# Squared ReLU with the square and the copy both on ScalarE, and the second product's halves stored apart and added at the end

## The chip, the cores and the metric

One core of a Trainium2 chip runs the whole kernel. The metric is the device time of one execution in microseconds (us). The time before is the median of three runs, 927.74 us. One further execution was profiled; all durations, waits and idle times below come from it.

## What is computed

The input x has 2048 rows of 640 numbers. Each row is normalised (layer norm without weights) to xn. Two branches read xn:

```
qkv = xn @ wqkv                        # 640 x 1920; 32 heads of 20
s   = softmax(mask(q k^T / sqrt(20))) v @ wo     # causal, window of 256
r   = relu(xn @ w1 + b1)               # 640 x 1536
y   = (r * r) @ w2 + b2                # 1536 x 640
out = x + s * silu(y)
```

All of it is in 32-bit floating point. The kernel keeps that precision with matrix products of rounded operands: an operand is split into a high part (its value rounded to the matrix engine's 32-bit format) and a low part (the rest), and a product is taken as high x high, high x low and low x high.

## The kernel before

**Stages.** A first stage normalises x, transposes it into `xT`, and computes v and the first q and k columns. Then a loop of 268 steps (`for s in range(steps)`) runs the attention, 16 head pairs by 16 row tiles, one tile a step. TensorE has time left in each step, and a generator `filler()` fills it with other products, one piece at a time: first the remaining q and k columns (`qkps`), then the MLP, at last the output product with wo (`out_filler`, tile `wops`), most of which runs after the attention has ended.

**One attention step** issues, for the head pair: scores (`sps`, TensorE) whose row maxima VectorE takes (`junk`, `mt`, L505); transposed scores (`stps`, TensorE, L540), which ScalarE exponentiates (`p`, L546) and GpSimd masks (`p`, L547 and L549); a step later ScalarE copies the result to 16 bits (`ph`, L554); a step after that VectorE computes what the copy lost (`pl`, L560); then TensorE multiplies both with v (`ops`). Every fourth step ScalarE also handles the row maxima (`mrow`, L518 and L519) and evacuates `ops` (`osb`, L596). The scores live in two single-bank tiles, the transposed scores in one tile of two banks with no second copy: the next `stps` waits until the `p` before it has been read out.

**The MLP** runs in eight blocks, `blocks`: the hidden columns are taken in two halves `hf` (0, then 1), and for each half the rows in four blocks `b` of 512. In a block there is first a stretch of six products into PSUM tiles `hps` (th x fp), each evacuated by `evac`: ScalarE takes the relu from PSUM (L971), ScalarE squares it into the high part `hh` (L972); the PSUM bank is then counted free. `later(1.2, rest)` puts off the rest: VectorE squares the relu in place (L976), GpSimd subtracts the high part to give the low part `hl` (L977). Then comes a stretch of eight products into tiles `yps` (four row tiles x two column halves), read from `hh` and `hl`. Their evacuation differs by half: for `hf` 0 ScalarE copies `yps` to `ysb` (L1011), and it is stored in DRAM as `y_d[0]`; for `hf` 1 VectorE adds to it the earlier half, read back into `yin` (L935, L1009), and the sum is stored as `y_d[1]`. The products `qkps`, `hps`, `yps` share three PSUM banks.

**The output stage** takes the rows in eight units of two row tiles. For a unit it loads the attention output `ob` and `y_d[1]` as `yb`; GpSimd adds the bias b2 (L1093), ScalarE takes silu (L1123); TensorE transposes `ob` and multiplies with wo in four groups `wops`; VectorE multiplies a group with `yb` (L1144) and GpSimd adds x, loaded as `xres` (L1145); the row tile is stored.

**What sets the order.** The order of instructions on each engine is fixed when the program is written: `clock` is the writer's own count of TensorE time, `later` and `soon` place deferred work by it, and each engine then runs its list strictly in that order. All transfers are issued by SyncE, also in one order; an issue that must wait holds up those behind it.

Of the kernel before, what the change touches and what calls it, by code (L numbers as in the profile page):

```python
# [9 lines left out]
F32 = mybir.dt.float32  # L10
# [3 lines left out]
AF = mybir.ActivationFunctionType  # L14
ALU = mybir.AluOpType

P = 128
S = 2048
D = 640
# [3 lines left out]
NT = S // P  # L23
KC = D // P
NP = H // 2
NB = 4
# [32 lines left out]
def attn_mlp_kernel(ctx: ExitStack, tc, x, wqkv, wo, w1, b1, w2, b2, out):  # L59
    nc = tc.nc  # L60
# [24 lines left out]
    y_d = [dram.tile([P, NT, D], F32, name=f"y{i}") for i in range(2)]  # L85
# [31 lines left out]
    wgt = ctx.enter_context(tc.tile_pool(name="wgt", bufs=2))  # L117
# [19 lines left out]
    with tc.tile_pool(name="ph1v", bufs=2) as p1v, tc.tile_pool(name="ph1", bufs=2) as p1, tc.tile_pool(name="ph1x", bufs=4) as p1b, tc.tile_pool(name="ph1w", bufs=1) as p1w, tc.tile_pool(name="ph1t", bufs=2, space=PSUM) as p1t:  # L137
        xts = {}
# [136 lines left out]
        with tc.manual_schedule(engines={E_.PE, E_.Activation, E_.DVE, E_.Pool, E_.SP}):  # L275
# [90 lines left out]
            for w in "kq":  # L366
                ps = pat.tile([P, BT // 2], F32, tag="s", name="qkps")
# [263 lines left out]
    def later(wait, fn):  # L631
        tasks.append((clock[0] + wait, len(tasks), fn))
# [254 lines left out]
    def filler():  # L887
# [37 lines left out]
        ensure("10")  # L925
        blocks = [(0, (b + NB - 1) % NB) for b in range(NB)] + [(1, (b + NB - 2) % NB) for b in range(NB)]
        last = len(blocks) - 1
        order = [4 * b + tt for hf, b in blocks if hf for tt in range(4)]
        yins = {}

        def load_yin(i):
            if i < NT:
                t = order[i]
                yins[t] = wgt.tile([P, D], F32, tag="wgkh", name="yin")
                nc.sync.dma_start(yins[t], y_d[0][:, t, :])  # L935
        xb, its = [xT[p][NB - 1] for p in range(2)], []

        for n, (hf, b) in enumerate(blocks):
            if n % NB == 0:
                ensure(f"1{hf}")  # L940
            if n == NB - 1:
                w1t[1] = queue_w1(1)
                w2t[1] = queue_w2(1)
                shut.update(("11", "21"))
            if n == last:
                wo_part = queue_wo()
                shut.add("o")
            ensure_bulk(its)
            wt1 = w1t[hf]()
            hs, made, nxt = {}, set(), []  # L950

            def used(n=n, b=b, nxt=nxt):
                if n == NB - 1:
                    shut.discard("11")
                if n == last:
                    shut.discard("o")
                if n < last and blocks[n + 1][1] != b:
                    nxt.extend(load_xb(blocks[n + 1][1]))
            for th in range(2):
                for fp in range(NFH // 2):  # L960
                    yield from room()
                    ps = Acc(BT, "hps")

                    def evac(ps=ps, th=th, fp=fp, hs=hs, made=made):
                        hh = [stg.tile([P, BT], F32R, tag="stg", name="hh"),
                              stg.tile([P, BT], F32R, tag="stg", name="hl") if fp == 0 else wgt.tile([P, D], F32R, tag=f"wg{'kq'[fp % 2]}l", name="hl")[:, :BT]]
                        hs[th, fp] = hh

                        vload[0] += 0.5
                        r = at2.tile([P, BT], F32, tag="relu", name="relu")  # L970
                        nc.scalar.activation(r, ps.tile, AF.Relu)  # L971
                        nc.scalar.activation(hh[0], r, AF.Square)  # L972
                        ps.free(0.9)

                        def rest():
                            nc.vector.tensor_mul(r, r, r)  # L976
                            nc.gpsimd.tensor_sub(hh[1], r, f32(hh[0]))  # L977
                            made.add((th, fp))
                        later(1.2, rest)
                    fi = hf * NFH + 2 * fp  # L980
                    job = open_job(evac, *([used] if (th, fp) == (1, NFH // 2 - 1) else []))
                    mms = [(i, lin1(wt1, (wp * KC + c) * FHALF + (2 * fp + i) * P, P), xb[xp][:, c * BT + th * MT:c * BT + (th + 1) * MT]) for i in range(2) for c in range(KC) for wp, xp in ((0, 0), (0, 1), (1, 0))]
                    for m, (i, w_, x_) in enumerate(mms):
                        halves(job, ps, w_, x_, m == 0, m == len(mms) - 1, i * MT, MT)
                        if m in (0, 3 * KC):
                            one_half(job, ps, i, b1s, pick[:, fi + i:fi + i + 1].to_broadcast([P, MT]), i * MT, MT)
                        yield 0.1065
            if n % NB == 0:
                ensure(f"2{hf}")
            if n == NB:  # L990
                load_yin(0)
                load_yin(1)
            wt2 = w2t[hf]()
            for tt in range(4):
                t = b * 4 + tt
                place = [None]
                jobs = []

                def start(nh, hf=hf, t=t, place=place, idx=4 * (n - NB) + tt, end=n == NB - 1 and tt == 3, n=n, tt=tt):
                    sl = slice(nh * HALF, (nh + 1) * HALF)  # L1000
                    ps = Acc(HALF, "yps")

                    def evac():
                        vload[0] += 0.5
                        if not nh:
                            place[0] = wgt.tile([P, D], F32, tag="wgqh", name="ysb")
                        ysb = place[0]
                        if hf:
                            nc.vector.tensor_add(ysb[:, sl], ps.tile, yins[t][:, sl])  # L1009
                        else:  # L1010
                            nc.scalar.activation(ysb[:, sl], ps.tile, AF.Copy)  # L1011
                        ps.free(1.2)
                        if nh:
                            post(y_d[hf][:, t, :], ysb)
                            if hf:
                                del yins[t]
                                load_yin(idx + 2)
                            if end:
                                shut.discard("21")
                    return [ps, open_job(evac), 0]  # L1020

                def product(jb, nh, fc):
                    ps, job, _ = jb
                    while (tt // 2, fc // 2) not in made:
                        if state[2] < 10 ** 6:
                            yield None
                        elif tasks:
                            finish()
                        else:
                            drain(backlog, 1)  # L1030
                    for hp, wp in ((0, 0), (0, 1), (1, 0)):
                        jb[2] += 1
                        halves(job, ps, hs[tt // 2, fc // 2][hp][:, fc % 2 * MT + tt % 2 * P:fc % 2 * MT + (tt % 2 + 1) * P], lin1(wt2, (wp * NFH + fc) * D + nh * HALF, HALF), jb[2] == 1, jb[2] == 3 * NFH)
                        yield 0.133
                for nh in range(2):
                    yield from room()
                    job = start(nh)
                    for fc in range(NFH):
                        yield from product(job, nh, fc)
                if n == last and tt % 2:  # L1040
                    load(0)
                    load(1)
            if n < last and nxt:
                xb, its = nxt
            else:
                its = []
# [33 lines left out]
        return wo_part  # L1080

    def out_filler(wo_part):
        oT, xts = {}, {}
        b2t = wgt.tile([P, D], F32, tag="wgkl", name="b2t")
        nc.sync.dma_start(b2t, b2.partition_broadcast(P))

        def load_res(t):
            xts[t] = wgt.tile([P, D], F32, tag="wgkh", name="xres")
            nc.sync.dma_start(xts[t], x[t * P:(t + 1) * P, :])

        def transposes(u):
            ob, yb = ld[u]
            nc.gpsimd.tensor_add(yb, yb, b2t.unsqueeze(1).to_broadcast([P, 2, D]))  # L1093
            big = bigp.tile([P, KC * BT], F32R, tag="big", name=f"oT_{u}")
            oT[u] = big.rearrange("p (s c n) -> p s c n", s=2, c=KC)
# [14 lines left out]
                pending.append(evac)  # L1110

        load_res(0)
        for u in range(2 * NB):
            while u not in ld:
                load(u)
# [8 lines left out]
            for t2 in range(2):  # L1124
# [3 lines left out]
                for nh in range(2):  # L1128
# [8 lines left out]
                    yield from mm_group(ps, mms, 0.133)  # L1137
                    if nh == 0 and t + 1 < NT:
                        load_res(t + 1)
                    load(u + 1)  # L1140
                    load(u + 2)

                    def evac(ps=ps, sl=sl, t2=t2, nh=nh, res=res, xt=xt, t=t, yb=yb):
                        nc.vector.tensor_mul(res[:, sl], ps, yb[:, t2, sl])  # L1144
                        nc.gpsimd.tensor_add(res[:, sl], res[:, sl], xt[:, sl])  # L1145
                        if t == NT - 1:
                            post(out[t * P:(t + 1) * P, sl], res[:, sl])
                        elif nh:
                            post(out[t * P:(t + 1) * P, :], res)
# [115 lines left out]
```

## Time and profile before

| | |
|---|---|
| median of the runs (lowest to highest) | 927.74 us (927.52 to 932.7) |
| the profiled execution | 931.02 us, of which 929.3 us is the span from its first to its last instruction |
| busy: TensorE products / weight loads | 895.5 us / 857.7 us |
| busy: VectorE / ScalarE / GpSimd | 723.1 / 625.7 / 592.5 us |
| the MLP | from 275 us (first `hps`) to 832 us (last `ysb`) |
| the output stage | from 832 us to the end |

In the rows of the profile, PE is TensorE's products and PEld its weight loads, DVE is VectorE, ACT ScalarE, POOL GpSimd, SP SyncE; a name with q is an engine's own queue. `out<-in` names the tiles written and read. Behind `|` stand busy us and the mean ns of one instruction, then the time for which the engine sat idle just before them and what ended it. A busy share is a mean over stages with different limits, and a wait is put down to the instruction that came last.

### The profile page before, as it was taken

The page shows a single profiled execution, that of the slowest core. Times are in us where ns is not written, and L with a number is a line of the kernel's source. Part 1 is how long each engine was busy: PE and PEld are TensorE (multiplying, and loading weights), DVE is VectorE, ACT ScalarE, POOL GpSimd, SP SyncE. Part 2 cuts the span into 40 slices and gives each one's busy share as a digit, 9 for nine tenths or more (in the row PEclk, how much of TensorE's full clock was granted, in tenths as well). Part 3 has the DMA queues.
Part 4 walks back from the last instruction along what each step waited for, and adds up shares of the span by engine and source line. Part 5 has one row for each costly group of instructions (what it writes and reads, how often), then busy time and mean ns, then how long its engine had stood idle before and what let it go on. Part 6 is the DMA issues. An engine that isn't in the chain of part 4 may idle for free.

```text
span 929.3 us, 35638 instructions
## 1 busy us (share of the span) xinstructions
PE 895.5 (96%) x14464; PEld 857.7 (92%) x14464; DVE 723.1 (78%) x1717; ACT 625.7 (67%) x1048; POOL 592.5 (64%) x863
## 2 busy tenths in 40 slices
PE   8999999999999999999999999999999999889998
PEld 8999999999888999899999898899999899889998
DVE  6874368999899978968978989989988988762332
ACT  4443338787888877877878787868777768762221
POOL 6010005676647877958968777968868868864654
PEclk9999999999999999999999999999999999997999
DMA  7897877679786263362454445374563471173773
GB/s 265 305 386 273 239 240 273 217 248 287 224 263 189 59 214 103 73 209 68 142 181 124 108 134 135 98 227 131 154 175 103 116 238 53 39 235 115 271 283 118
DMA packets 105419, 169.97 MB, mean 183 GB/s; under 512 B 41336, under 2 KB 58920, under 8 KB 102696
## 3 DMA queue, kind: packets, MB, share of 16 engines
q1 hardware_dynamic: 105256, 167.70, 57.3%
q8 instruction: 114, 1.87, 0.9%
q14 instruction: 49, 0.40, 0.1%
HBM read 96.17 MB, written 70.91 MB: 180 GB/s over the span
## 4 chain that ended last, share of the span: by engine, by line
PE 69%; DVE 10%; issue 8%; POOL 5%; ACT 5%; DMA 3%; DVEq 0%; POOLq 0%; ACTq 0%; SPq 0%
PE yps L487 12%; PE ops L487 10%; PE hps L487 10%; PE qkps L487 9%; PE wops L655 8%; PE vps L232 8%; PE sps L497 5%; DVE junk L505 4%; PE stps L540 4%; PE qkps L209 3%; DVE pl L560 2%; ACT p L546 2%; POOL p L549 1%; POOL p L547 1%; DMA qs<-mrow 1%
## 5 line engine op out<-in xcount | busy, mean ns | idle before, releaser
L505 DVE CUSTOM_DVE_ANT_0 junk<-sps,mask 128x384 bf16<-128x384 f32 (+2 forms) x512 | 270.8, 529 | 73.1 <-PE sps L497 30.2
L546 ACT ACTIVATE p<-stps,ebias 128x768 f32<-128x768 f32 (+2 forms) x256 | 219.0, 856 | 113.3 <-PE stps L540 76.2
L560 DVE TENSOR_TENSOR pl<-p,ph 128x768 f16<-128x768 f32 (+2 forms) x256 | 273.1, 1067 | 12.2 <-PE ops L487 8.1
L547 POOL TENSOR_SCALAR_AFFINE_SELECT p<-p 128x256 f32<-128x256 f32 x256 | 173.0, 676 | 155.7 <-ACT p L546 150.1
L487 PE MATMUL yps<-w,hh 64*128 64x320 f32 x1536 | 253.8, 316 | 10.6 <-DVE ysb L1009 6.4
L487 PE MATMUL hps<-xb,w 64*128 64x256 f32 x2520 | 238.9, 285 | 0.6 <-issue 0.5
L487 PEld LDWEIGHTS hps<-xb,w 64*128 64x128 f32 x2520 | 224.9, 187 | 1.2 <-issue 0.6
L554 ACT ACTIVATE ph<-p 128x768 f16<-128x768 f32 (+2 forms) x256 | 203.2, 794 | 26.1 <-POOL p L549 25.0
L487 PEld LDWEIGHTS yps<-w,hh 64*128 64x128 f32 x1536 | 194.3, 186 | 15.0 <-DVE ysb L1009 8.0
L487 PE MATMUL ops<-vp,ph 64*128 64x61 bf16 x2880 | 201.8, 189 | 0.1
L487 PE MATMUL ops<-vp,pl 64*128 64x61 bf16 x2880 | 199.9, 188 | 0.3 <-DVE pl L560 0.3
L487 PE MATMUL yps<-w,hl 64*128 64x320 f32 x768 | 187.7, 314 | 0.0
L487 PEld LDWEIGHTS <-ph 64*128 64x128 f16 x2880 | 174.4, 94 | 4.9 <-PE sps L497 1.1
L487 PEld LDWEIGHTS <-pl 64*128 64x128 f16 x2880 | 175.5, 94 | 0.6 <-DVE pl L560 0.5
L497 PE MATMUL sps<-ks,qs 60*128 60x384 f32 (+2 forms) x512 | 127.6, 360 | 9.1 <-DVE mt L505 8.3
L549 POOL TENSOR_SCALAR_AFFINE_SELECT p<-p 128x256 f32<-128x256 f32 x224 | 129.1, 576 | 0.0
L487 PEld LDWEIGHTS yps<-w,hl 64*128 64x128 f32 x768 | 120.5, 186 | 0.0
L540 PE MATMUL stps<-qs,ks 62*128 62x384 f32 (+2 forms) x512 | 112.8, 345 | 3.2 <-DMA qs<-mrow 1.6
L487 PE MATMUL qkps<-xT,wgkh 64*128 64x512 f32 x320 | 102.5, 398 | 0.0
L487 PE MATMUL qkps<-xT,wgqh 64*128 64x512 f32 x320 | 102.3, 397 | 0.0
L497 PEld LDWEIGHTS sps<-ks,qs 60*128 60x128 f32 x512 | 70.5, 185 | 22.3 <-DVE mt L505 20.6
L540 PEld LDWEIGHTS stps<-qs,ks 62*128 62x128 f32 x512 | 67.2, 187 | 6.9 <-issue 2.6
(120 smaller groups left out, 1721.1 us busy)
## 6 DMA issues: line engine op xcount, KB each, us to landing
ks<-k_d SPq DMA_DIRECT2D x64, 240.0 KB
qs<-q_d SPq DMA_DIRECT2D x64, 240.0 KB
xb<-xs SPq DMA_DIRECT2D x12, 1280.0 KB
xs<-xT SPq DMA_DIRECT2D x8, 1280.0 KB
y<-ysb SPq DMA_DIRECT2D x32, 320.0 KB
k_d<-shm SPq DMA_DIRECT2D x19, 512.0 KB
q_d<-shm SPq DMA_DIRECT2D x19, 512.0 KB
v_d<-vt SPq DMA_DIRECT2D x8, 976.0 KB
```

The lines of the kernel that those rows point to most:

```text
L209: nc.tensor.matmul(ps, wt[:, c, :], xT[part][b][:, c * BT + t0:c * BT + t0 + n], start=m == 1, stop=m == 3 * KC)
L232: nc.tensor.matmul(ps, xT[xp][b][:, c * BT + t * P: c * BT + (t + 1) * P], wv[wp][:, c, nh * HALF:(nh + 1) * HALF], start=first and m == 0 ...
L487: return nc.tensor.matmul(out, a[r], b_[r], skip_group_check=True, **kw)
L497: nc.tensor.matmul(ss[hh][:, :nk], qs[i][o, q * P:(q + 1) * P], ks[i][o, k0 * P:k0 * P + nk], start=True, stop=True)
L505: nc.vector.tensor_tensor_reduce(out=junk[:, :nk], in0=ss[hh][:, :nk], in1=mask[:, 3 * P - nk:], scale=1.0, scalar=-3.0e38, op0=ALU.add, o ...
L540: nc.tensor.matmul(tps[:, hh, :n], ks[i][o, kb * P:(kb + 1) * P], qs[i][o, kb * P:kb * P + n], start=True, stop=True)
L546: nc.scalar.activation(p32[:, :, :n], tps[:, :, :n], AF.Exp, scale=SCALE, bias=ebias)
L547: nc.gpsimd.affine_select(p32[:, :, 0:P], p32[:, :, 0:P], pattern=[[0, 2], [1, P]], compare_op=ALU.is_ge, fill=0.0, base=0, channel_multip ...
L549: nc.gpsimd.affine_select(p32[:, :, 2 * P:], p32[:, :, 2 * P:], pattern=[[0, 2], [-1, P]], compare_op=ALU.is_gt, fill=0.0, base=0, channel ...
L554: nc.scalar.activation(ph[:, :, :n], p32[:, :, :n], AF.Copy)
L560: nc.vector.tensor_sub(pl[:, :, :n], p32[:, :, :n], ph[:, :, :n])
L655: nc.tensor.matmul(ps, a, b_, start=j == 0, stop=j == n - 1)
```

## The change

ScalarE now takes three instructions at each of the 48 evacuations of `hps`: the relu, the square (in place, 32-bit) and a copy that rounds it to the high part. VectorE no longer squares. The deferred part comes 0.4 us instead of 1.2 us of the writer's clock after the relu and now holds the square and the copy. ScalarE evacuates both halves of the second product, so `y_d[1]` holds the second half alone. The first half is read back only in the output stage: two loads of 128 x 640 for each unit into new tiles `y0`, and two more additions on GpSimd ahead of the bias. There the addition of x moves from GpSimd to VectorE.

```diff
-        order = [4 * b + tt for hf, b in blocks if hf for tt in range(4)]
-        yins = {}
-        def load_yin(i):
-            ...
-                nc.sync.dma_start(yins[t], y_d[0][:, t, :])
...
                         r = at2.tile([P, BT], F32, tag="relu", name="relu")
                         nc.scalar.activation(r, ps.tile, AF.Relu)
-                        nc.scalar.activation(hh[0], r, AF.Square)
                         ps.free(0.9)

                         def rest():
-                            nc.vector.tensor_mul(r, r, r)
+                            nc.scalar.activation(r, r, AF.Square)
+                            nc.scalar.activation(hh[0], r, AF.Copy)
                             nc.gpsimd.tensor_sub(hh[1], r, f32(hh[0]))
                             made.add((th, fp))
-                        later(1.2, rest)
+                        later(0.4, rest)
...
                         ysb = place[0]
-                        if hf:
-                            nc.vector.tensor_add(ysb[:, sl], ps.tile, yins[t][:, sl])
-                        else:
-                            nc.scalar.activation(ysb[:, sl], ps.tile, AF.Copy)
+                        nc.scalar.activation(ysb[:, sl], ps.tile, AF.Copy)
                         ps.free(1.2)
                         if nh:
                             post(y_d[hf][:, t, :], ysb)
-                            if hf:
-                                del yins[t]
-                                load_yin(idx + 2)
...
+        def load_y0(u):
+            y0s[u] = [wgt.tile([P, D], F32, tag="wgql", name="y0") for _ in range(2)]
+            for t, y0 in enumerate(y0s[u]):
+                nc.sync.dma_start(y0, y_d[0][:, 2 * u + t, :])
...
         def transposes(u):
             ob, yb = ld[u]
+            for t, y0 in enumerate(y0s.pop(u)):
+                nc.gpsimd.tensor_add(yb[:, t], yb[:, t], y0)
             nc.gpsimd.tensor_add(yb, yb, b2t.unsqueeze(1).to_broadcast([P, 2, D]))
...
         load_res(0)
+        load_y0(0)
...
                     if nh == 0 and t + 1 < NT:
                         load_res(t + 1)
+                    if (t2, nh) == (0, 1) and u + 1 < 2 * NB:
+                        load_y0(u + 1)
...
                         nc.vector.tensor_mul(res[:, sl], ps, yb[:, t2, sl])
-                        nc.gpsimd.tensor_add(res[:, sl], res[:, sl], xt[:, sl])
+                        nc.vector.tensor_add(res[:, sl], res[:, sl], xt[:, sl])
```

TensorE's list has the same instructions in the same order in both programs. The other lists move. ScalarE, in the first stretch of block 4, between two exponentials (`p`) of which the first also has the row maxima and `osb` behind it; before:

```order
L546 ACTIVATE p_14185<-stps,ebias 128x768
L518 ACTIVATE mrow<-stps 8x128
L519 ACTIVATE mrow<-mrow 8x128
L971 ACTIVATE relu<-hps 128x512
L972 ACTIVATE hh<-relu 128x512
L596 ACTIVATE osb<-ops 128x488
L554 ACTIVATE ph<-p_14109 128x768
L546 ACTIVATE p_14277<-stps,ebias 128x768
```

and changed:

```order
L546 ACTIVATE p_14185<-stps,ebias 128x768
L518 ACTIVATE mrow<-stps 8x128
L519 ACTIVATE mrow<-mrow 8x128
L963 ACTIVATE relu<-hps 128x512
L967 ACTIVATE relu<-relu 128x512
L968 ACTIVATE hh<-relu 128x512
L596 ACTIVATE osb<-ops 128x488
L554 ACTIVATE ph<-p_14109 128x768
L546 ACTIVATE p_14273<-stps,ebias 128x768
```

One instruction of 128 x 512 more stands ahead of `osb`, `ph` and the next `p`. In the changed list 13 of the 48 evacuations have their square and copy between two `p` that also have `mrow` and `osb` between them.

VectorE, at the first evacuations of block 0 (`p`, `ph` and `pl` belong to the attention):

```order
 L505 ISA junk,mt_100<-sps,mask 128x384
 L505 ISA mt_100 128x1
-L976 TENSOR_TENSOR relu<-relu 128x512
 L560 TENSOR_TENSOR pl<-p_5461,ph 128x768
 L505 ISA junk,mt_100<-sps,mask 128x384
```

The square is gone from between a row maximum and the `pl` behind it; nothing takes its place.

SyncE, in the output stage, the issues of one unit; before:

```order
L1089 DMA xres<-in_A_x_dram 128x640
L1065 DMA ob_21391<-o_87 128x2x640
L1066 DMA yb_21392<-y_84 128x1280
L620 DMA out_dram<-res 128x640
```

and changed (`y_83` is the stored first half, `y_21397` and `y_21398` are the new tiles):

```order
L1077 DMA xres<-in_A_x_dram 128x640
L1048 DMA ob_21377<-o_87 128x2x640
L1049 DMA yb_21378<-y_84 128x1280
L1073 DMA y_21397<-y_83 128x640
L1073 DMA y_21398<-y_83 128x640
L620 DMA out_dram<-res 128x640
```

The two new loads are queued behind `ob` and `yb`, which are for the unit after the next, while they themselves are for the next one.

More of the change, by code (lines that the diff above doesn't have):

```diff
@@ L927, in filler @@
         last = len(blocks) - 1
-        order = [4 * b + tt for hf, b in blocks if hf for tt in range(4)]
-        yins = {}
-        def load_yin(i):
-            if i < NT:
-                t = order[i]
-                yins[t] = wgt.tile([P, D], F32, tag="wgkh", name="yin")
-                nc.sync.dma_start(yins[t], y_d[0][:, t, :])
         xb, its = [xT[p][NB - 1] for p in range(2)], []
@@ L997, in filler, with start @@
                 jobs = []
-                def start(nh, hf=hf, t=t, place=place, idx=4 * (n - NB) + tt, end=n == NB - 1 and tt == 3, n=n, tt=tt):
+                def start(nh, hf=hf, t=t, place=place, end=n == NB - 1 and tt == 3, n=n, tt=tt):
                     sl = slice(nh * HALF, (nh + 1) * HALF)
@@ L1082, in out_filler @@
     def out_filler(wo_part):
-        oT, xts = {}, {}
+        oT, xts, y0s = {}, {}, {}
         b2t = wgt.tile([P, D], F32, tag="wgkl", name="b2t")
         nc.sync.dma_start(b2t, b2.partition_broadcast(P))
+        def load_y0(u):
+            y0s[u] = [wgt.tile([P, D], F32, tag="wgql", name="y0") for _ in range(2)]
+            for t, y0 in enumerate(y0s[u]):
+                nc.sync.dma_start(y0, y_d[0][:, 2 * u + t, :])
         def load_res(t):
```

3 lines of the change are left out of this document (removed).

## The prediction

> **What bounds the kernel now.** I read the page's busy shares and its chain of work first, then what TensorE waits for in the MLP, then the busy time of each engine by stretch.
>
> ```profile
> span 929.3 us, 35638 instructions
> PE 895.5 (96%) x14464; PEld 857.7 (92%) x14464; DVE 723.1 (78%) x1717; ACT 625.7 (67%) x1048; POOL 592.5 (64%) x863
> PE 69%; DVE 10%; issue 8%; POOL 5%; ACT 5%; DMA 3%; DVEq 0%; POOLq 0%; ACTq 0%; SPq 0%
> ```
>
> TensorE is busy for 96% of the span and carries 69% of the chain. No instruction of TensorE is added, removed or moved by this change, so the time can only change through how long TensorE stands waiting. The waits of its weight loads from 275 to 833 us, the MLP (engine and line that waited, releaser: total us, times, longest):
>
> ```profile
> PEld sps L497 <- DVE mt L505: 15.8, 37, 1.2
> PEld yps L487 <- DVE ysb L1009: 8.0, 6, 3.9
> PEld yps L487 <- ACT ysb L1011: 4.1, 7, 1.0
> PEld yps L487 <- ACT relu L971: 2.6, 4, 1.5
> PEld stps L540 <- ACT mrow L518: 2.6, 5, 0.6
> PEld stps L540 <- ACT p L546: 1.2, 4, 0.5
> ```
>
> VectorE makes TensorE wait 15.8 + 8.0 = 23.8 us, ScalarE 4.1 + 2.6 + 2.6 + 1.2 = 10.5 us. So all that VectorE could give back is 2.6% of the span. Why VectorE is late, and whether ScalarE has room, is read from the first stretches of the eight blocks (here block 4 and the sum of all eight), then from the second stretches of the first and of the last four blocks:
>
> ```profile
> core 0: us, PE busy (x) PEld busy (x) DVE busy (x) ACT busy (x) POOL busy (x), PEclk, DMA share, GB/s
> 559.00:598.00 39.00, 36.43 (x710) 34.19 (x706) 36.42 (x76) 32.65 (x54) 31.76 (x44) 0.96 0.35 91
> sum 287.00, PE 278.02 PEld 266.76 DVE 260.57 ACT 238.94 POOL 244.04; mean PE 34.75 PEld 33.35 DVE 32.57 ACT 29.87 POOL 30.50
> ...
> sum 129.00, PE 124.31 PEld 119.91 DVE 104.87 ACT 100.41 POOL 91.36; mean PE 31.08 PEld 29.98 DVE 26.22 ACT 25.10 POOL 22.84
> ...
> sum 127.00, PE 119.93 PEld 116.09 DVE 103.49 ACT 83.84 POOL 89.28; mean PE 29.98 PEld 29.02 DVE 25.87 ACT 20.96 POOL 22.32
> ```
>
> In the first stretches VectorE is busy 260.57 of 287 us, 91%, ScalarE 83%, GpSimd 85%. That is where the change takes from VectorE and gives to ScalarE.
>
> **The change, part by part.** The prices, from the groups by line:
>
> ```profile
> L971 ACT ACTIVATE relu<-hps 128x512 f32<-128x512 f32 x48 | 27.9, 580 | 0.3 <-PE hps L487 0.3
> L972 ACT ACTIVATE hh<-relu 128x512 fp32r<-128x512 f32 x48 | 30.3, 632 | 1.5
> L976 DVE TENSOR_TENSOR relu<-relu 128x512 f32<-128x512 f32 x48 | 38.3, 799 | 4.0 <-ACT hh L972 3.6
> L1009 DVE TENSOR_TENSOR ysb<-yps,yin 128x320 f32<-128x320 f32 x32 | 15.4, 481 | 6.0 <-PE yps L487 3.1 <-DMA y<-ysb 2.8
> L1011 ACT ACTIVATE ysb<-yps 128x320 f32<-128x320 f32 x32 | 13.4, 420 | 0.0
> ```
>
> *VectorE loses the squares:* 48 x 0.799 = 38.3 us. In the first stretches its load falls from 260.57 to 222 us, 77%. The row maximum that TensorE waits for is queued behind less, but a `pl` still has to wait for ScalarE's `ph`, which will come later than now. Bounds: nothing back, or all of the 15.8 us. I take a little over half, **-9**: 14 points of load are taken away, but the later `ph` gives a part back.
>
> *VectorE loses the second half's evacuation:* 32 additions of 0.481 become 32 copies of 0.420 on ScalarE, which in those stretches goes from 83.84 to 97.3 of 127 us, 77%. That is what it carries in the first four blocks (100.41/129 = 78%), where the same copies cost 4.1 us of waiting against 8.0 us for the additions. Bounds: 0 to -8; **-4**.
>
> *ScalarE gains one instruction an evacuation.* The square stays; the copy is new. The nearest row is L972 with 632 ns, and as it must wait for the square I add 0.04 us: 48 x 0.67 = 32 us. In the first stretches that makes 238.94 + 32 = 271 of 287 us, 94%: ScalarE takes the place that VectorE has at 91%. Whether TensorE feels it depends on how late an exponential may be. The exponentials in the MLP, the transposed scores, and one step of ScalarE in block 4 in order of time:
>
> ```profile
> L546 ACT ACTIVATE p<-stps,ebias 128x768 f32<-128x768 f32 x204 | 174.2, 854 | 89.2 <-PE stps L540 60.5 <-PE stps L512 24.4 <-DVE pl L560 2.4
> L540 PE MATMUL stps<-qs,ks 62*128 62x384 f32 x448 | 101.1, 357 | 3.2 <-DMA qs<-mrow 1.6 <-ACT mrow L518 1.3 <-ACT p L546 0.2
> ...
> 589.84 0.90 ACT L546 ACTIVATE p<-stps,ebias 128x768 f32<-128x768 f32 x1 [0.39 <-PE stps L512]
> 590.64 0.25 ACT L518 ACTIVATE mrow<-stps 8x128 f32<-8x128 f32 x1
> 590.92 0.31 ACT L519 ACTIVATE mrow<-mrow 8x128 fp32r<-8x128 f32 x1
> 591.14 0.57 ACT L971 ACTIVATE relu<-hps 128x512 f32<-128x512 f32 x1
> 591.75 0.63 ACT L972 ACTIVATE hh<-relu 128x512 fp32r<-128x512 f32 x1
> 592.28 0.56 ACT L596 ACTIVATE osb<-ops 128x488 f32<-128x488 f32 x1
> 592.74 0.83 ACT L554 ACTIVATE ph<-p 128x768 f16<-128x768 f32 x1
> 593.47 0.89 ACT L546 ACTIVATE p<-stps,ebias 128x768 f32<-128x768 f32 x1
> ```
>
> 204 exponentials in 558 us make a step of 2.73 us. A step holds 0.36 us of `stps` and 0.90 us of `p`; as `stps` has one tile only, the rest, about 1.4 us, is how late `p` may be before TensorE stands. In the step shown `p` to `p` takes 593.47 - 589.84 = 3.63 us: already 0.9 us late. With the copy it is 4.30, 1.57 late: TensorE stands, and `ph` and `osb` behind the copy are late by 0.67 too. The changed order has 13 such steps. Priced in full they cost 13 x 0.67 = 8.7 us. The other 35 evacuations have no `mrow` and `osb`: 3.63 - 1.0 + 0.67 = 3.3 us from `p` to `p`, 0.6 late, mostly hidden; 0.12 us each, 4.2 us, for those that meet a queue already late. Together **+13**. Bounds: 0, if the 89.2 us for which ScalarE sat waiting ahead of `p` take it all, and +32, if none of it is hidden. A check by likeness: the waits of `stps` for ScalarE are 2.6 + 1.2 = 3.8 us now and would be 16.8 us with ScalarE at 94%; VectorE at 91% costs 15.8.
>
> The Trainium skill's page ScalarE: Activation LUTs, section Rules for kernel authors, speaks against this part: it sends multiplications to VectorE and budgets about 0.3 us and 0.83 ns an element for an ACTIVATE. As an estimate from that page an instruction of 512 would take 0.72 us, the 48 copies 35 us instead of 32; this case's trace has 0.632 us, and the sum would be 1 us higher by the page.
>
> *The relu queues behind another evacuation's copy, and the bank it frees is late:* the 2.6 us of waits for `relu` grow; 0 to +5, **+2**. GpSimd's `hl` keeps its length; it waits for ScalarE instead of VectorE.
>
> *The output stage.* GpSimd gives up 32 additions of 0.876 us and gets 16 of 128 x 640; VectorE gets 32. Rows: the additions, GpSimd's price for 128 x 640, and around one unit the last load's issue, silu and the multiplication that needs it; then the last addition, and the stage's load.
>
> ```profile
> L1145 POOL TENSOR_TENSOR res<-res,xres 128x320 f32<-128x320 f32 x32 | 27.8, 876 | 35.1 <-DVE res L1144 35.1
> L1093 POOL TENSOR_TENSOR yb<-yb,b2t 128x1280 f32<-128x1280 f32 x8 | 23.6, 2952 | 3.4 <-PE yps L487 3.4
> L188 POOL TENSOR_TENSOR wv<-wvr,wv 128x640 fp32r<-128x640 f32 x5 | 7.7, 1567 | 0.0
> 869.57 0.44 SPq L1066 DMA_DIRECT2D yb<-y  x1
> 862.86 1.29 ACT L1123 ACTIVATE yb<-yb 128x1280 f32<-128x1280 f32 x1
> 869.05 0.49 DVE L1144 TENSOR_TENSOR res<-wops,yb 128x320 f32<-128x320 f32 x1 [1.88 <-PE wops L655]
> 925.52 0.86 POOL L1145 TENSOR_TENSOR res<-res,xres 128x320 f32<-128x320 f32 x1 [1.26 <-DVE res L1144]
> 850.00:929.00 79.00, 74.66 (x558) 73.98 (x558) 25.85 (x52) 17.14 (x27) 44.86 (x40) 0.99 0.60 210
> ```
>
> The new loads go out behind the `yb` of 869.57, at 870. With 4 to 6 us for `ob`, `yb` and themselves at the 210 GB/s of the stage or a little above, two additions of 1.57, the bias 2.95 and silu 1.29, `yb` is ready at 881.4 to 883.4. The unit it is for starts its multiplications one unit of 9.9 us after 869.05, at 879. VectorE is 2 to 4 us late; three PSUM banks let TensorE run on for two groups of 2.2 us. So TensorE just does not stand, with nothing to spare: 0 to +5, I take **+1**. At the very end the addition on VectorE, about 0.48 us, replaces 0.86: **-0.4**.
>
> The sum: -9 - 4 + 13 + 2 + 1 - 0.4 = **+2.6 us**. The profiled execution, 931.0 us with its span of 929.3, would become 933.6; it lies 3.3 us over the median, so on the median the forecast is 927.7 + 2.6 = **930.3 us**.
>
> Beside the sum stands the clock, by stretch (it is the value after POOL's busy time):
>
> ```profile
> 572.40:575.80 3.40, 3.40 (x34) 3.40 (x33) 2.83 (x9) 2.24 (x5) 1.61 (x3) 0.50 1.03 251
> 835.20:848.90 13.70, 12.63 (x84) 11.76 (x85) 3.94 (x9) 3.30 (x6) 5.49 (x5) 0.50 0.37 126
> ```
>
> After stalls the granted clock was halved for 3.4 us, and for 13.7 us where the output stage begins. One such 3.4 us more or less is worth 1.7 us; I count none.
>
> **The rivals.** *ScalarE becomes the bound (slower).* In block 4's first stretch, where weights are split as well, ScalarE has 32.65 + 6 x 0.67 = 36.7 of 39 us. If a late `ph` also holds VectorE's `pl`, and with it the next row maximum, the relief of 9 us shrinks to 2 and the 13 become 20: -2 - 4 + 20 + 4 + 1 - 0.4 = +18.6, **946 us**. It decides once the exponentials are over 1.4 us late in every third step. For it: 94%, and one tile for `stps`. Against it: 89.2 us of idle time ahead of `p`.
>
> *VectorE's relief pays (faster).* ScalarE's idle time takes the copies but for 3 us, 14 of the 15.8 us come back and 6 of the 8: -14 - 6 + 3 + 1 - 0.4 = -16.4, **911 us**. For it: VectorE is the fullest engine now. Against it: the copies fall into the very stretches where ScalarE has 17% left. The Trainium skill's GPSIMD Engine Reference, section Specifications, speaks for it: GpSimd shares its memory interfaces with VectorE instructions that have two inputs there, and the squares are such. By that rule GpSimd's masks would shorten as well; no row here separates it.
>
> *The output stage waits for the stored halves (slower).* If the loads need 10 us, TensorE stands 3 us in each of the six later units, less the 1 counted: **947 us**.
>
> *The moved order does nothing:* if the waits merely change their names, **928 us**; this lies within my forecast's own range.
>
> **How the numbers follow.** Forecast (near balance, 919 to 937): 0.47. ScalarE the bound: 0.29. Output stage: 0.06. VectorE's relief: 0.18. A measurement of this kernel can tell about 1%, 9.3 us, from no change: faster than 918.5 has 0.18, slower than 937 has 0.35, between 0.47. The range goes from 912 to 948 and takes in the sums of both larger rivals but for the outer half of the faster one.
>
> **What would show it.** Right: `sps` waits for `mt` fall to about 7 us between 275 and 833; `stps` waits for `p` and `mrow` grow from 3.8 to over 12; VectorE at 75 to 80% and ScalarE over 92% in the first stretches; no waits of `wops` for `res` after 850. Wrong: if `stps` waits stay under 6 us, the copies were hidden and the time falls; if `sps` waits stay over 12, VectorE was late for another reason than its squares.

## The result: slower by 1.5%, a faster MLP and a slower output stage

| | median, us | ratio to before (95% interval) |
|---|---|---|
| before | 929.23 (4 runs, taken beside the change) | |
| changed | 943.62 (4 runs) | 1.0146 (1.0106 to 1.0185) |

The profiled execution of the changed kernel took 944.62 us with a span of 942.5; before, 931.02 and 929.3. One execution of the first experiment's kernel ran at a granted clock of 0.654 and took 1175.99 us; no number below rests on it.

From the page of the changed kernel, the busy shares and the chain:

```profile
PE 897.6 (95%) x14464; PEld 860.5 (91%) x14464; DVE 692.2 (73%) x1669; ACT 661.9 (70%) x1128; POOL 568.8 (60%) x847
PE 63%; ACT 11%; POOL 7%; issue 7%; DVE 5%; DMA 5%; SPq 1%; ACTq 0%; DVEq 0%; POOLq 0%
```

VectorE's part of the chain fell from 10% to 5%, ScalarE's rose from 5% to 11%, GpSimd's from 5% to 7%. Where the 13.2 us of span came from is seen by cutting at the start of the last evacuation of `yps`, the end of the MLP. The evacuations of the second half before, then all of them in the changed kernel (count, shortest/median/longest ns, first and last start):

```profile
L1009 DVE TENSOR_TENSOR ysb<-yps,yin x32: 444/484/492, 603.5 to 831.8; 128x320 f32<-128x320 f32 x32
```

```profile
L997 ACT ACTIVATE ysb<-yps x64: 409/427/440, 323.3 to 822.3; 128x320 f32<-128x320 f32 x64
```

The MLP ends 9.5 us earlier. The stage behind it, before and changed, by engine (busy us, mean granted clock, DMA share, GB/s):

```profile
831.80:929.30 97.50, 89.93 (x671) 87.74 (x671) 33.73 (x62) 23.48 (x37) 54.73 (x46) 0.92 0.55 191
```

```profile
822.30:942.50 120.20, 96.77 (x671) 92.25 (x671) 53.76 (x92) 24.29 (x38) 52.05 (x30) 0.89 0.57 200
```

The same 671 products take 22.7 us longer, 120.20 instead of 97.50. GpSimd's work fell, from 54.73 to 52.05 us. VectorE's grew by 20 us with the additions of x, but it is busy for only 53.76 of 120.20 us, and the same additions cost no time in the kernel before (an experiment below). So the 22.7 us are waits. The waits from 835 us to the end in the changed kernel (total us, times, longest):

```profile
ACT yb L1114 <- POOL yb L1083: 73.9, 8, 17.3
DVE res L1137 <- ACT yb L1114: 35.1, 4, 10.6
POOL yb L1082 <- DMA y<-y: 24.7, 4, 11.7
POOL yb L1082 <- PE wops L655: 22.7, 2, 12.1
PE wops L655 <- DVE res L1137: 13.9, 5, 4.7
PEld wops L655 <- DVE res L1137: 12.5, 4, 5.0
```

Read from the bottom: TensorE's products wait for VectorE's multiplication, as it frees their bank; that waits for silu on ScalarE, that for GpSimd's bias addition, and GpSimd for the loads of the stored first half (`y<-y`). Two more of GpSimd's waits, 22.7 us, end by the profile with a product into `wops`; that the loads held these too is likely but not shown. One unit of it in order of time (start, duration, in brackets the idle time before and what ended it):

```profile
882.61 0.48 SPq L1049 DMA_DIRECT2D yb<-y  x1
883.19 0.87 SPq L1073 DMA_DIRECT2D y<-y  x2
...
891.65 3.09 POOL L1082 TENSOR_TENSOR yb<-yb,y 128x640 f32<-128x640 f32 x2 [11.71 <-DMA y<-y]
894.82 2.90 POOL L1083 TENSOR_TENSOR yb<-yb,b2t 128x1280 f32<-128x1280 f32 x1
...
897.75 1.27 ACT L1114 ACTIVATE yb<-yb 128x1280 f32<-128x1280 f32 x1 [13.56 <-POOL yb L1083]
...
899.05 0.49 DVE L1137 TENSOR_TENSOR res<-wops,yb 128x320 f32<-128x320 f32 x1 [10.16 <-ACT yb L1114]
```

The loads are issued at 883.2 and GpSimd can start at 891.65, 8.5 us later. Additions, bias and silu take 7.4 us more. VectorE stood for 10.16 us.

In the MLP the waits did change sides, as the diff suggests. Weight loads from 275 to 840 us in the changed kernel:

```profile
PEld stps L540 <- ACT p L546: 8.9, 16, 1.0
PEld yps L487 <- ACT ysb L997: 7.8, 14, 2.6
PEld sps L497 <- DVE mt L505: 5.9, 14, 0.6
PEld yps L487 <- ACT relu L963: 3.1, 5, 1.0
```

and the first stretches of the eight blocks, summed:

```profile
sum 281.00, PE 273.32 PEld 263.69 DVE 232.39 ACT 259.02 POOL 232.42; mean PE 34.16 PEld 32.96 DVE 29.05 ACT 32.38 POOL 29.05
```

ScalarE is now the fullest of the three, 259.02 of 281 us, 92%; VectorE fell to 83%. Yet the waits for VectorE's row maxima fell by 9.9 us and those for the exponentials rose by only 7.7.

### The profile page after: what moved, and what is told of

Read it like the earlier page. It is cut to its first block, busy times and chain, and to the rows that moved or that the text cites. A ratio compares the mean times of both kernels' runs of the same rounds, so it can differ in the third digit from the quotient of the medians.

```text
span 942.5 us, 35654 instructions
## 1 busy us (share of the span) xinstructions
PE 897.6 (95%) x14464; PEld 860.5 (91%) x14464; DVE 692.2 (73%) x1669; ACT 661.9 (70%) x1128; POOL 568.8 (60%) x847
## 4 chain that ended last, share of the span: by engine, by line
PE 63%; ACT 11%; POOL 7%; issue 7%; DVE 5%; DMA 5%; SPq 1%; ACTq 0%; DVEq 0%; POOLq 0%
PE hps L487 11%; PE yps L487 10%; PE qkps L487 10%; PE ops L487 9%; PE vps L232 7%; PE sps L497 4%; PE stps L540 4%; PE wops L655 3%; PE qkps L209 3%; ACT p L546 3%; ACT ph L554 2%; DMA y<-y 2%; DVE junk L505 2%; POOL yb L1082 2%; DMA qs<-mrow 2%
## 5 line engine op out<-in xcount | busy, mean ns | idle before, releaser
L560 DVE TENSOR_TENSOR pl<-p,ph 128x768 f16<-128x768 f32 (+2 forms) x256 | 259.9, 1015 | 24.3 <-ACT ph L554 9.0
L547 POOL TENSOR_SCALAR_AFFINE_SELECT p<-p 128x256 f32<-128x256 f32 x256 | 164.4, 643 | 159.2 <-ACT p L546 158.5
L549 POOL TENSOR_SCALAR_AFFINE_SELECT p<-p 128x256 f32<-128x256 f32 x224 | 122.9, 549 | 0.0
L497 PE MATMUL sps<-ks,qs 60*128 60x384 f32 (+2 forms) x512 | 117.5, 354 | 4.7 <-DVE mt L505 4.4
L540 PE MATMUL stps<-qs,ks 62*128 62x384 f32 (+2 forms) x512 | 108.0, 345 | 7.1 <-ACT p L546 4.6
L655 PE MATMUL wops<-wo,oT 128*128 128x320 f32 x384 | 71.2, 338 | 16.6 <-DVE res L1137 13.9
L655 PEld LDWEIGHTS wops<-wo,oT 128*128 128x128 f32 x384 | 64.3, 210 | 19.3 <-DVE res L1137 12.5
```

Source lines behind the costliest of these rows:

```text
L497: nc.tensor.matmul(ss[hh][:, :nk], qs[i][o, q * P:(q + 1) * P], ks[i][o, k0 * P:k0 * P + nk], start=True, stop=True)
L540: nc.tensor.matmul(tps[:, hh, :n], ks[i][o, kb * P:(kb + 1) * P], qs[i][o, kb * P:kb * P + n], start=True, stop=True)
L547: nc.gpsimd.affine_select(p32[:, :, 0:P], p32[:, :, 0:P], pattern=[[0, 2], [1, P]], compare_op=ALU.is_ge, fill=0.0, base=0, channel_multip ...
L549: nc.gpsimd.affine_select(p32[:, :, 2 * P:], p32[:, :, 2 * P:], pattern=[[0, 2], [-1, P]], compare_op=ALU.is_gt, fill=0.0, base=0, channel ...
L560: nc.vector.tensor_sub(pl[:, :, :n], p32[:, :, :n], ph[:, :, :n])
L655: nc.tensor.matmul(ps, a, b_, start=j == 0, stop=j == n - 1)
```

## The experiments

**Theories.** (1) Taking the squares from VectorE sped the MLP up; the stored halves, loaded too late, slowed the output stage by more. (2) The MLP gained by the copies of the second half's `yps`, and the output stage is slow for GpSimd's longer chain, not for the loads. (3) As predicted: the MLP near balance. Ratios are to the kernel before, run on the same chip.

**The two halves of the change, alone.** First only the evacuation of `hps`:

```diff
-                        nc.scalar.activation(hh[0], r, AF.Square)
                         ps.free(0.9)

                         def rest():
-                            nc.vector.tensor_mul(r, r, r)
+                            nc.scalar.activation(r, r, AF.Square)
+                            nc.scalar.activation(hh[0], r, AF.Copy)
...
-                        later(1.2, rest)
+                        later(0.4, rest)
```

> Only the evacuation of hps is changed (square and copy on ScalarE, 0.4 instead of 1.2); evacuation of yps and output stage as before. Theory 1, the MLP was sped up by taking the squares from VectorE and the output stage lost more by the late stored halves: the last ysb comes at 823 to 826 us instead of 832, the stage behind it keeps its 97 us, the median falls by 6 to 9 us (ratio 0.990 to 0.994). Theory 2, the MLP was sped up by the copies of the second half's yps on ScalarE: the last ysb stays at 830 to 834, the median within 3 us of before. Theory 3, as predicted, ScalarE's load eats the relief: the median 2 to 6 us over before.

Measured: 918.37 us (median of three), 0.9887 (0.9851 to 0.9924), a little more than theory 1 allowed. The profile is of a further execution:

> The first experiment's kernel once more, for a profile at full clock. Expected: span 916 to 918, last product into yps at 820 to 823 us, waits of sps for mt 5 to 8 us and of stps for p 8 to 12, as in the changed kernel; the output stage at full clock or with one halved stretch.

This execution took 913.8 us, with a span of 912.1, less than the 916 to 918 expected. Its evacuations, its waits and its output stage:

```profile
L1009 DVE TENSOR_TENSOR ysb<-yps,yin x32: 446/484/494, 596.9 to 819.3; 128x320 f32<-128x320 f32 x32
...
PEld stps L540 <- ACT p L546: 9.0, 16, 1.0
PEld sps L497 <- DVE mt L505: 5.9, 14, 0.6
PEld yps L487 <- DVE ysb L1009: 5.0, 6, 3.0
...
819.30:912.10 92.80, 85.80 (x671) 84.00 (x671) 31.35 (x63) 23.42 (x37) 53.97 (x46) 0.98 0.58 202
```

The last `ysb` starts at 819.3, 3 us ahead of that of the changed kernel, with VectorE still adding the second half. (Profiles of one and the same MLP differ by up to 3 us at this place, so the ratios carry the verdict.) The output stage, which is the old one here, takes 92.80 us. In the profiles of the four later experiments on the MLP that keep it, it takes 92.8 to 93.6, so the 97.50 us before are 4 to 5 us more than usual: the clock was halved for 13.7 us at the start of the stage there, for 3.4 to 6.8 us in these. Against the usual stage the change costs not 22.7 but about 27 us. Then the rest of the change, with the old evacuation of `hps`:

> Only the other half of the change: yps always copied by ScalarE, the first half loaded and added in the output stage, x added by VectorE; hps evacuated as before. Theory 1: the last ysb at 827 to 832 us, the output stage 118 to 122 us long, the median 17 to 23 us over before. Theory 2: the last ysb at 821 to 825, the output stage as long as in the changed kernel, the median 10 to 14 us over before. If the output stage were long only because the MLP ended early (the same work pressed into a later place), it would be 100 to 105 us here.

Measured: 955.92 us, 1.0286 (1.0244 to 1.0327), 27 us, more than the 17 to 23 of theory 1. The last `ysb` is at 830.8 against 831.8, and the stage behind it:

```profile
831.00:952.60 121.60, 97.15 (x671) 92.96 (x671) 53.42 (x92) 23.96 (x38) 52.12 (x30) 0.87 0.57 197
```

So the copies of `yps` gave the MLP about 1 us, less than single profiles differ by, and not what theory 2 says. The output stage is just as long behind a late MLP as behind an early one. The two ratios multiply to 1.017; the whole change has 1.0146 (1.0106 to 1.0185). Theory 3 falls, and so does the MLP half of theory 2; its other half, GpSimd's chain, is tested next.

**Loads or GpSimd's chain?** The changed kernel with one number changed:

```diff
-                    if (t2, nh) == (0, 1) and u + 1 < 2 * NB:
+                    if (t2, nh) == (0, 0) and u + 1 < 2 * NB:
                         load_y0(u + 1)
```

As `load(u + 2)` follows in the same place, the two loads now stand ahead of `ob` and `yb` for the unit after the next.

> The changed kernel with the two loads of the stored first half issued one group earlier, ahead of the loads of ob and yb for the unit after the next. If the output stage waits for those loads because they are queued behind 1.3 MB that is not needed yet, they land 3 to 5 us earlier, the waits of GpSimd for them (34 us) fall by more than half and the median falls by 8 to 16 us against the changed kernel. If GpSimd's longer chain (two more additions ahead of the bias and silu) is the bound, the waits for the loads shrink but the median falls by less than 4 us.

Measured: 923.17 us, 0.9938 (0.9914 to 0.9963): 20 us under the changed kernel. Its output stage, and a load with the addition that waits for it:

```profile
820.60:921.20 100.60, 89.68 (x671) 86.23 (x671) 57.13 (x92) 24.23 (x38) 53.22 (x30) 0.95 0.69 239
...
882.25 0.90 SPq L1073 DMA_DIRECT2D y<-y  x2
...
886.13 3.34 POOL L1082 TENSOR_TENSOR yb<-yb,y 128x640 f32<-128x640 f32 x2 [5.17 <-DMA y<-y]
```

3.9 us from issue to use instead of 8.5. The median fell by more than the 8 to 16 us expected, GpSimd's waits for the loads by less than half, from 34.1 to 26.4 us in all. But GpSimd now starts early enough: the waits of VectorE's multiplication for silu fell from 35.1 to 14.4 us, and those of TensorE's products for that multiplication from 13.9 to 0.2. Next the loads were left out for all units but the first:

```diff
-            y0s[u] = [wgt.tile([P, D], F32, tag="wgql", name="y0") for _ in range(2)]
-            for t, y0 in enumerate(y0s[u]):
+            y0s[u] = y0s[0] if u else [wgt.tile([P, D], F32, tag="wgql", name="y0") for _ in range(2)]
+            for t, y0 in enumerate([] if u else y0s[u]):
                 nc.sync.dma_start(y0, y_d[0][:, 2 * u + t, :])
...
-            for t, y0 in enumerate(y0s.pop(u)):
+            for t, y0 in enumerate(y0s[u]):
                 nc.gpsimd.tensor_add(yb[:, t], yb[:, t], y0)
```

> The changed kernel with the stored first half loaded for the first unit of the output stage only; GpSimd's additions all stay and add that unit's tiles again, so the first half of the other units is wrong. If the late loads are all of the output stage's loss, the median is 20 to 25 us under the changed kernel, at 919 to 924. If GpSimd's longer chain costs as well, more than 927.

Measured: 922.71 us, 0.9939 (0.9916 to 0.9961). Seven units without loads are no better than loads in time. So about 20 us of the loss are the loads' place in the queue. Some 5 us are left against the first experiment (918.37), and they are hardly chance: on the same chip all six runs with the early loads (921.5 to 925.1) lie above its three (917.58 to 919.32). GpSimd's longer chain is the likely cause, as it isn't the loads: the last version below has no such additions in the output stage, and its median is 4.5 us less than this one's on the same chip. The two output stages, first without the loads, then without the additions:

```profile
819.80:921.00 101.20, 89.73 (x671) 86.82 (x671) 69.09 (x92) 24.55 (x38) 52.95 (x30) 0.93 0.55 191
```

```profile
821.10:914.00 92.90, 84.59 (x671) 82.55 (x671) 57.52 (x92) 23.81 (x38) 29.45 (x15) 0.99 0.61 210
```

Theory 1 stands, with a small part for GpSimd's chain.

**What the squares and the copies cost, each alone.** VectorE's squares left out with nothing in their place; GpSimd subtracts the high part from the relu itself:

```diff
                         def rest():
-                            nc.vector.tensor_mul(r, r, r)
                             nc.gpsimd.tensor_sub(hh[1], r, f32(hh[0]))
```

> The kernel before without VectorE's squares and with nothing in their place; left out is the square in the low part (GpSimd subtracts the high part from the relu itself). It measures the relief term alone, which the prediction put at -9 us (bounds 0 and -15.8). Theory A, the relief was undersized and ScalarE's cost about right: 18 to 24 us faster. Theory B, the relief was about right and ScalarE's copies cost almost nothing: 8 to 13 us faster. Theory C, both are small and the gain of the square's move comes from the earlier place of the deferred part: less than 5 us faster.

Measured: 906.44 us, 0.9776 (0.9754 to 0.9798), 21 us. The waits for VectorE in it:

```profile
PEld sps L497 <- DVE mt L505: 5.7, 13, 0.9
PEld yps L487 <- DVE ysb L1008: 5.5, 7, 3.1
```

The row maxima's waits fell by 10.1 us, nearly the 9 of the prediction. All rows of the weight loads' waits in the MLP together fell by 15 us, from 39.6 to 24.5.

One more instruction on ScalarE, the squares kept:

```diff
                         def rest():
+                            nc.scalar.activation(hh[0], r, AF.Square)
                             nc.vector.tensor_mul(r, r, r)
```

> The kernel before with VectorE's squares kept and one more ScalarE instruction of 128x512 in each deferred part (the square into the high part is taken twice). It measures the cost of the copies alone, which the prediction put at +13 us (bounds 0 and +32). Theory A: 9 to 14 us slower. Theory B: 0 to 4 us slower. As VectorE's square here waits for the second of the two, up to 2 us of this may be VectorE's.

Measured: 947.71 us, 1.0213 (1.0189 to 1.0236), 20 us. That is over the range of theory A, and the waits of VectorE and of TensorE's weight loads show another path than the one that was to be priced:

```profile
DVE relu L977 <- ACT hh L976: 41.3, 39, 2.4
...
PEld sps L497 <- DVE mt L505: 36.6, 66, 1.8
PEld stps L540 <- ACT p L546: 0.8, 3, 0.4
```

The exponentials are no later for TensorE (0.8 us). But VectorE's square overwrites the relu and must wait until ScalarE has read it, 41.3 us in all against 3.6 before, and the row maxima queued behind it wait with it. The experiment so measured a coupling, not ScalarE's load. Two more runs separate them. The first experiment with the deferred part at 1.2 has the copies and nothing on VectorE behind them:

> The evacuation of hps alone, as in the first experiment (square and copy on ScalarE), but the deferred part at 1.2 instead of 0.4 of the writer's clock. Against the kernel without VectorE's squares (906 us) it has only ScalarE's copies more, and nothing on VectorE that waits for them: the difference is the copies' own cost. If that is what the prediction put down (13 us): 918 to 921. If the 20 us of the doubled square came through VectorE's square waiting for ScalarE: 5 to 10 us, 911 to 916, and the place at 0.4 costs the rest. If the place at 0.4 helps: over 922.

Measured: 916.44 us, 0.986 (0.9834 to 0.9885). Against the kernel without squares (906.44, 0.9776) it is 8 to 10 us slower, by ratios or medians. That is the copies' cost, together with ScalarE's square coming later: in this kernel it stands in the deferred part too. The place at 0.4 instead of 1.2 can't be told from nothing: the two intervals overlap. And the kernel before with only the place moved:

> The kernel before with only the deferred part moved from 1.2 to 0.4 of the writer's clock; VectorE still squares, and now stands sooner behind ScalarE's square. If VectorE's coupling to ScalarE is what the squares cost, its waits for hh grow over 3.6 us, those of sps for mt over 15.8, and the median rises by 3 to 12 us. If only the squares' work counts: within 2 us of before.

Measured: 936.14 us, 1.007 (1.0045 to 1.0095).

```profile
DVE relu L976 <- ACT hh L972: 26.1, 31, 1.9
...
PEld sps L497 <- DVE mt L505: 24.6, 53, 1.2
```

With no instruction added anywhere, squares that come sooner behind ScalarE cost 7 us: their waits for ScalarE went from 3.6 to 26.1 us, those for the row maxima from 15.8 to 24.6. That is the coupling.

**Smaller parts, and a better version.** The addition of x on VectorE, alone:

```diff
-                        nc.gpsimd.tensor_add(res[:, sl], res[:, sl], xt[:, sl])
+                        nc.vector.tensor_add(res[:, sl], res[:, sl], xt[:, sl])
```

> The kernel before with nothing changed but the addition of x in the output stage, on VectorE instead of GpSimd. Every theory: 0 to 1 us faster (the last addition 0.49 instead of 0.86 us), not to be told from no change. If VectorE's addition with two operands in SBUF is held up by GpSimd's additions next to it (0.79 us in the changed kernel, 0.49 at its shortest), single additions beside yb are longer, without any wait of TensorE.

Measured: 927.88 us, 0.9985 (0.9967 to 1.0003), not to be told from no change. And a version that keeps the change's MLP but adds the first half where it was added before, on GpSimd:

```diff
-                        if hf:
-                            nc.vector.tensor_add(ysb[:, sl], ps.tile, yins[t][:, sl])
-                        else:
-                            nc.scalar.activation(ysb[:, sl], ps.tile, AF.Copy)
+                        nc.scalar.activation(ysb[:, sl], ps.tile, AF.Copy)
                         ps.free(1.2)
                         if nh:
+                            if hf:
+                                nc.gpsimd.tensor_add(ysb, ysb, yins[t])
```

(with the first experiment's evacuation of `hps` and x added by VectorE)

> A version to beat both: square and copy on ScalarE as in the change, both halves of yps copied by ScalarE, but the first half read back beside the product as in the kernel before and added there by GpSimd, one addition of 128x640 a row tile; x added by VectorE. By the runs so far: the MLP as in the changed kernel (last ysb at 820 to 824 us), the output stage 97 us or a little less, the median 914 to 920. If GpSimd's 16 additions of 1.6 us in the second stretches delay its masks and with them ph, up to 5 us more.

Measured: 918.21 us, 0.9888 (0.987 to 0.9907). It beats both kernels, and so does the plainer one of the first experiment with the deferred part at 1.2, 0.986; the two can't be told apart.

## Why the prediction was right or wrong

The time, 943.6 us, lies in the range, on the side of its slower cases, and that is luck. The likeliest case, near balance at 930.3, did not come: the sum gave +2.6 us and +14.4 were measured. Two large errors of opposite sign hid each other: the MLP gained 10 us where +2 were forecast, and the output stage lost about 27 where +0.6 were.

- **VectorE loses the squares (-9, bounds 0 and -15.8): mis-sized, -21.** The step that failed is the bound. I took the weight loads' 15.8 us of waits for row maxima as all that could come back. These did fall about as forecast, by 10.1 us without the squares. But other waits fell by 5 more, among them those of `yps` for `ysb` (VectorE's from 8.0 to 5.5, ScalarE's from 4.1 to 2.7). The profile without the squares also has no halved clock in the MLP, where the one before has two such stretches of 3.4 us, worth up to 1.7 each. The last 2 to 3 us stay open.
- **ScalarE gains the copies (+13, with +2 for late banks): too large by a third or more, 8 to 10.** The mechanism was right: `stps` waits for `p` went from 1.2 to 8.9 us, and ScalarE rose to 92% in the first stretches. The check by likeness gave too much, 16.8 us of `stps` waits for ScalarE; with `mrow` they were 8.9 + 0.8. A slip in the working changed nothing: a step holds two products into `stps`, 101.1 us in 224 steps or 0.45 us each, not 0.36, and the slack is still about 1.4.
- **The second half's evacuation (-4): nothing that can be told apart.** With this part alone the waits for `ysb` fell from 8.0 + 4.1 to 9.5 us, but the MLP ended only 1 us earlier, and profiles of one MLP differ by up to 3.
- **The output stage (+1, bound +5): mis-sized, about +27** (22.7 between the two profiles, 27 by the medians of the experiment with this half alone). The failed step is the 4 to 6 us for landing, and it failed in the arithmetic: `ob` and `yb` with 655 kB each and the two loads with 328 kB each are 1.97 MB, which at the 210 GB/s that I named take 9.4 us. With 9.4 the same working gives `yb` at 886.7, 7.7 us after the multiplication could start at 879, 3.3 more than two groups cover, and 20 us over six units. Measured were 8.5 us, in a stretch in which the 16 DMA engines were full, a share of 0.97 at 332 GB/s. That is 2.8 MB, as stores of `out` and loads of x are among it; so the corrected figure is near by chance, with too few bytes at too low a rate:

```profile
883.20:891.60 8.40, 8.40 (x60) 8.40 (x59) 3.80 (x8) 0.99 (x3) 0.00 (x0) 1.00 0.97 332
```

  The rival that named this place, the output stage at 947 us, had a chance of 0.06; it was the one that came, with part of the faster MLP of another rival beside it. About 20 us are the loads' place in the queue; some 5 more go, as far as is known, with GpSimd's longer chain.
- **The last addition (-0.4):** can't be told from nothing, 0.9985 (0.9967 to 1.0003).
- **What would show it.** `sps` waits of 7 us: 5.9. `stps` waits for ScalarE over 12: 8.9 + 0.8, less. VectorE at 75 to 80%: 83%. ScalarE over 92%: 92%. No waits of `wops` for `res` after 850: 13.9 us of the products and 12.5 us of the weight loads, the sign that the step was wrong.

**The shared interface.** The prediction let the Trainium skill's GPSIMD Engine Reference, section Specifications, speak for the faster rival: GpSimd shares its memory interfaces with VectorE's instructions that have two inputs in SBUF, the on-chip memory. The runs agree where VectorE adds x beside GpSimd's additions: in the run with that addition alone it took 0.787 us in the mean, while the multiplication just ahead of it, with one of its inputs in PSUM, took 0.490.

```profile
L1145 DVE TENSOR_TENSOR res<-res,xres 128x320 f32<-128x320 f32 x32 | 25.2, 787 | 1.1
L1144 DVE TENSOR_TENSOR res<-wops,yb 128x320 f32<-128x320 f32 x32 | 15.7, 490 | 22.4 <-PE wops L655 22.4
```

The order of time separates the two cases. In the changed kernel 23 of the 32 additions ran while GpSimd stood idle and took 0.49 us each. The nine that began while one of GpSimd's additions ran took 1.14 to 2.69 us, and the multiplication took 0.47 to 0.49 either way. In the run with x on VectorE alone this cost no time. GpSimd's masks did shorten, from 676 to 643 ns in the mean, here before and in the changed kernel; but where the squares were left out with nothing in their place they took 665, and 686 where the MLP was as before. So most of the shortening does not follow the squares, and what causes it stays open.

```profile
L547 POOL TENSOR_SCALAR_AFFINE_SELECT p<-p 128x256 f32<-128x256 f32 x256 | 173.0, 676 | 155.7 <-ACT p L546 150.1
```

```profile
L547 POOL TENSOR_SCALAR_AFFINE_SELECT p<-p 128x256 f32<-128x256 f32 x256 | 164.4, 643 | 159.2 <-ACT p L546 158.5
```

## What to carry to other kernels

The waits that a profile lists for one tile are no bound for what a relief gives: here 15.8 us were listed, 10.1 of them went, and the time fell by 21. When an instruction waits for another engine, everything queued behind it waits too: placing VectorE's squares 0.8 us of the writer's clock sooner behind ScalarE cost 7 us with no instruction added. A load for the next unit must not be queued behind prefetches for the unit after it: the order of two issues was worth 20 us. And bytes ahead of a load, divided by the rate that the stage shows, say whether it is hidden; the bytes of everything else in the queue belong to it.

## What was not expected of the hardware

The granted clock turned small changes of waits into time. Before, the 3.4 us ahead of the halved stretch at 572.4 were these:

```profile
569.00:572.40 3.40, 2.11 (x45) 1.54 (x45) 3.26 (x8) 0.96 (x2) 2.81 (x5) 1.00 0.42 126
```

TensorE was busy 2.11 of 3.40 us, and for the next 3.4 the clock was halved. The Trainium skill's TensorE: Matmul & The Clock Gate, section Part 1: The HAM clock gate, puts the halved clock after at least one idle window of about 3.4 us; here it followed a window that was only partly idle, so the measurement decides. The busy share alone does not say when it happens. Two stretches of the same length, each with the one behind it, the first pair before and the second in the changed kernel:

```profile
398.30:401.70 3.40, 1.85 (x22) 1.47 (x20) 2.45 (x8) 1.30 (x3) 1.68 (x4) 1.00 0.98 339
401.70:405.10 3.40, 3.40 (x79) 3.32 (x79) 0.85 (x3) 2.01 (x3) 0.77 (x2) 1.00 0.58 163
```

```profile
396.60:400.00 3.40, 1.88 (x21) 1.39 (x20) 2.53 (x6) 0.90 (x2) 1.16 (x3) 1.00 0.88 297
400.00:403.40 3.40, 3.40 (x49) 3.40 (x46) 0.00 (x0) 1.63 (x2) 0.77 (x2) 0.50 0.57 146
```

TensorE was busy for 1.85 and 1.88 us, less than in the stretch above. Before, the clock stayed full; in the changed kernel it was halved. What else decides it these runs do not show.

In the output stage the mean clock was 0.92 over 97.50 us before and 0.89 over 120.20 us after. As an estimate from these rows, in time lost against full clock (0.08 x 97.50 = 7.8 and 0.11 x 120.20 = 13.2), that is 5.4 of the 22.7 us; the rest is the waits themselves.
